# Layer 3's last output projection in row form, a two-descriptor store, and identity matmuls ahead of the last V quarter

## The chip, the cores and the metric

One core of one Trainium2 chip runs the whole program. The metric is the device time of one execution in microseconds. The span that a profile gives runs from the first to the last instruction and is 1.7 to 2.2 us shorter than that time. In the lines of a profile, PE is the matrix engine (PEld its loads of the stationary operand), DVE the vector engine, ACT the scalar engine, SPq the sync engine's DMA queue; L637 is a line of the kernel, x16 a count, and square brackets hold how long the engine idled before and what ended it. PSUM is the memory that the matmuls of this kernel write to. The granted clock is the share of its full clock that PE was given; here it is 1.00 or 0.50 at any moment.

## The reference

Four attention layers (weights and caches A, B, A, B), for one token:

```python
x = x + attention_A(layernorm(x)); x = x + attention_B(layernorm(x))     # twice
# attention: q = (x @ wq) as 32 heads of 192; scores over 8192 cached keys; softmax;
#            o = p @ v; return o.reshape(1, 1, 32 * 192) @ wo             # wo: 6144 x 640
```

All inputs are bf16; x has 640 elements. K and V of one layer are 201 MB, so the program is a stream of loads with work beside it.

## The kernel before

The heads go in 16 pairs. The output projection of a layer goes in three blocks of wo, each for five pairs; the third is split in layers 1 and 3 into a first part ("wo", 10 of 15 slices) and "wob" (5 slices), and the last pair has its own slices, "wol" (3). The sum of all of them stays in PSUM as a column block: element 5p + c of the row of 640 sits in partition p, column c. Cut to what the change touches:

```python
def busy(n):                                     # n identity matmuls, 128x128 by 128x512, result unused
    PE.wait(ev_const, last["S"][0])
    for i in range(n):
        PE.op(... matmul(SP_[0][:, :], lhsT=ident[:], rhs=ident broadcast to 512) ..., signal=False, bank=Su[0])

def project(n, w, o, ev_o):
    t3 = w.rearrange("p (i n) -> p i n", n=D)
    PE.wait(ev_o, need(n), last["YB"])
    for i in range(k):
        for c in range(DC):                      # DC = 5: one moving column each
            e = PE.op(... matmul(YB[:, c:c + 1], lhsT=t3[:, i, c:D:DC], rhs=o[:, i:i + 1], ...), bank=YBu)
# values(): in the last pair of layers 1 and 3 the second half of V comes as two quarters
            if p == NPAIR - 1 and i == rounds // 4 and quarters(("v", nl, np_, u)):
                PE.wait(need(("vq", l)))         # the last quarter of V
# end of layer 3
            return None, DV.op(lambda v: v.tensor_tensor(x_bf[:], x_true[:], YB[:, 0:DC], ALU.add), ev_y, ev_true, bank=YBu)
e = SP.op(lambda s: s.dma_start(out[0, 0].rearrange("(p c) -> p c", c=DC), x_bf[:]), ev_true, sem=semOUT, inc=16)
```

`op(..., bank=...)` makes an engine wait for the last work of every other engine on that bank. After the last V quarter these things follow, one upon another: sixteen V matmuls, two vector operations that pick the heads apart, twelve fp32 matmuls that turn the result, wob and wol, the sum with x, the store.

Of the kernel before, what the change touches and what calls it, by code (L numbers as in the profile page):

```python
# [4 lines left out]
ACT = mybir.ActivationFunctionType  # L5
ALU = mybir.AluOpType
AX = mybir.AxisListType
BF16 = mybir.dt.bfloat16
# [60 lines left out]
def build(nc, A_x, A_k, A_v, A_wq, A_wo, B_x, B_k, B_v, B_wq, B_wo, out):  # L69
    _, H, SK, DH = A_k.shape  # L70
    D = A_x.shape[-1]
    P = 128
# [25 lines left out]
    with ExitStack() as ctx:  # L98
        def sb(name, shape, dt):
            return ctx.enter_context(nc.sbuf_tensor(name, shape, dt))  # L100

        def ps(name, n=1):
            return ctx.enter_context(nc.psum_tensor(name, [P, 512 * n], F32))
# [40 lines left out]
        vs = col(1)  # L144
        rs = col(1)
        xb = sb("xb", [P, DC], BF16)

        QM = ps("QM")
        SP_ = [ps("S0"), ps("S1")]
        OY = ps("OY", 4)  # L150
        O = OY[:, 0:VK * DH]
        YB = OY[:, VK * DH:]
        TB = ps("TB")
        use = {b: {} for b in ("QM", "S0", "S1", "O", "TB", "YB")}
        QMu, Ou, TBu, YBu = [(use[b],) for b in ("QM", "O", "TB", "YB")]
# [17 lines left out]
                                        base=0, pattern=[[-1, P]], channel_multiplier=1), e)  # L173
        PO.op(lambda g: g.memset(ones[:], 1.0))
        PO.op(lambda g: g.memset(one_b[:], 1.0))
        mask = acc[:, 0:2 * VK].rearrange("p (h i) -> p h i", h=2)
        e = PO.op(lambda g: g.memset(mask, 0.0))
        for t in range(G):
# [156 lines left out]
        def quarters(n):  # L335
            return n[0] == "v" and n[2:] == (NPAIR - 1, 1) and NB[n[1]] > 0
# [51 lines left out]
        def need(n):  # L388

            while n not in landed:  # L390
                m = plan[issued[0]]
                issued[0] += 1
                landed[m] = transfer(m)
            return landed[n]
# [45 lines left out]
        def layer(l, ev_z, ev_true):  # L440
# [82 lines left out]
            def project(n, w, o, ev_o):  # L523

                t3 = w.rearrange("p (i n) -> p i n", n=D)
                k = t3.shape[1]
                PE.wait(ev_o, need(n), last["YB"])
                for i in range(k):
                    for c in range(DC):
                        e = PE.op(lambda t, i=i, c=c, f=y_first[0], fin=n[0] == "wol" and i == k - 1: t.matmul(  # L530
                            YB[:, c:c + 1], lhsT=t3[:, i, c:D:DC], rhs=o[:, i:i + 1], start=f, stop=fin,
                            skip_group_check=True), signal=(i == k - 1 and c == DC - 1), bank=YBu)
                        y_first[0] = False
                if n[0] == "wo" and (n[2] < 2 or NB[l] == 0):
                    freed[n] = e
                return e

            def columns(k):

                PE.wait(last["row_written"], last["TT"], ev_const)  # L540
                for i in range(k):
                    e = PE.op(lambda t, i=i: t.matmul(TB[:, i:i + 1], lhsT=orow[:, i:k * P:k], rhs=one_b[96:97, :],
                                                      start=True, stop=True), signal=(i == k - 1), bank=TBu)
                last["orow"] = freed[n] = e
                last["TT"] = AC.op(lambda a: a.activation(oT[:, 0:k], TB[:, 0:k], ACT.Copy),  # L545
                                   e, last["oT"], bank=TBu)
# [55 lines left out]
            def values(p, us=(0, 1)):  # L602

                par = (l * NPAIR + p) % 2
                nl, np_ = first_load("v", l, p)
                k = 2 if p == NPAIR - 1 else VK
                N = min(512, k * DH)
                PE.wait(ev_p[p])
                if 0 in us:
                    PE.wait(last["rl"])  # L610
                    if p < NPAIR - 1:
                        e = PE.op(lambda t: t.matmul(TB[96:97, C_L:C_L + 2], lhsT=ones[:, 0:1], rhs=l_col[par][:],  # L612
                                                     start=True, stop=True), bank=TBu)
                    else:
                        for h in range(2):
                            e = PE.op(lambda t, h=h: t.matmul(TB[64 * h:64 * h + 64, C_L:C_L + 1], lhsT=ones[:, 0:1].broadcast_to([P, 64]),
                                                              rhs=l_col[par][:, h:h + 1], start=True, stop=True),
                                      signal=h == 1, bank=TBu)
                    last["lc"][par] = ev_l[p] = e
                PE.wait(last["O"])  # L620
                rounds = J // k // G
                for r in range(us[0] * rounds // 2, (us[-1] + 1) * rounds // 2):
                    u, i = divmod(r, rounds // 2)
                    u = turn[nl, np_][u]
                    PE.wait(need(("v", nl, np_, u)))
                    t = slot[place[("v", nl, np_, u)]]
                    if p == NPAIR - 1 and i == rounds // 4 and quarters(("v", nl, np_, u)):
                        PE.wait(need(("vq", l)))
                    for c in range(k * DH // N):
                        for g in range(G):  # L630
                            j = (i * G + g) * k
                            o, x, y = (O[32 * g:32 * g + 2 * k, c * N:(c + 1) * N],
                                       p_sb[par][:, u * JU + j:u * JU + j + k, :].rearrange("p j h -> p (j h)"),
                                       t[:, j * DH + c * N:j * DH + (c + 1) * N])
                            f, fin = r == 0, r == rounds - 1
                            e = PE.op(lambda t, c=c, g=g, o=o, x=x, y=y, f=f, fin=fin: (
                                t.matmul(o, lhsT=x, rhs=y, start=f, stop=fin) if c == 0 else  # L637
                                matmul_held(t, o, x, y, f, fin, 32, 32 * g)),
                                signal=(fin and c == k * DH // N - 1 and g == G - 1), bank=Ou)
                if 1 not in us:  # L640
                    return
                ev_O[p] = last["p"][par] = e
                if not stays("v", l, p):
                    for u in range(2):
                        freed[("v", nl, np_, u)] = e
# [37 lines left out]
            for n in [n for n in steps if n[1] == l]:  # L683
                if n[0] == "m":
                    products(*n[2:])
                elif n[0] == "s":
                    softmax(n[2])
                elif n[0] == "v":
                    values(n[2], n[3:] or (0, 1))
                elif n[0] == "e":  # L690
                    gather(n[2])
                elif n[0] == "busy":
                    busy(n[2])
                elif n[0] == "wqr":
                    q_rows(n[2], 1)
                elif n[0] == "wq":
                    q_rows(n[2], 0, 1 if l == 2 and n[2] == 0 else None)
                    q_ready = n[2] == 2 or q_ready
                elif n[0] == "wc":
                    columns(NW)  # L700
                    last["oTw"] = last["TT"]
                elif n[0] == "wo":
                    k = NW - NB[l] if n[2] == 2 else NW
                    last["oT"] = project(n, slot[place[n]][:, 0:k * D], oT[:, 0:k], last["oTw"])
                elif n[0] == "wob":
                    last["oT"] = freed[("wo", l, 2)] = project(
                        n, slot[place[("wo", l, 2)]][:, (NW - NB[l]) * D:NW * D], oT[:, NW - NB[l]:NW], last["oTw"])
                else:
                    last["TT"] = last["TTn"]
                    last["oTl"] = ev_y = project(n, rows[:], oTl, last["TTn"])  # L710
                    if l == 1:
                        busy(2)
                if q_ready and (n[0] == "wq" and l >= 2 or n[0] == "m" and n[3] == 1):
                    following = n[2] + 1 if n[0] == "m" else 1
                    if following < NPAIR and following not in ev_q:
                        q_spread(following)
                ahead()
            if l + 1 == NL:
                return None, DV.op(lambda v: v.tensor_tensor(x_bf[:], x_true[:], YB[:, 0:DC], ALU.add), ev_y, ev_true, bank=YBu)
            ev_z = DV.op(lambda v: v.tensor_tensor(z[:], xc[:], YB[:, 0:DC], ALU.add), ev_y, ev_xc, bank=YBu)  # L720
            e = DV.op(lambda v: v.tensor_tensor(x_true[:], x_true[:], YB[:, 0:DC], ALU.add), ev_y, ev_true, bank=YBu)
            last["YB"] = e
# [1 line left out]

        for l in range(NL):
            ev_z, ev_true = layer(l, ev_z, ev_true)
        e = SP.op(lambda s: s.dma_start(out[0, 0].rearrange("(p c) -> p c", c=DC), x_bf[:]), ev_true, sem=semOUT, inc=16)
        SP.wait(e)
        assert issued[0] == len(plan)

# [51 lines left out]
```

## Time and profile before

| | before |
|---|---|
| time, median of 3 runs at first (of 6 with the later ones) | 1984.8 us (1984.76) |
| DMA engines, queue 1's share of the span | 99.5% |
| last V quarter lands | 1975.10 us |
| from there to the issue of the store | 5.43 us |
| from the issue of the store to the end of the span | 3.07 us |

The number that matters is not in any share of busy time: it is the **tail**, the 8.5 us between the landing of the last V quarter and the end of the span. All before that is set by transfers.

### The profile page before, as it was taken

How to read it: one execution, taken by the hardware profiler on the slowest of the kernel's cores; microseconds unless marked ns; L12 is line 12 of the kernel's file. 1: busy time of each engine (PE TensorE's matmuls, PEld its weight loads, DVE VectorE, ACT ScalarE, POOL GpSimd, SP SyncE). 2: the span in 40 equal slices, each digit the busy share in tenths (PEclk: the TensorE clock that was granted, in tenths of full speed). 3: DMA queues.
4: the chain of work that ended last, by engine and by line, in shares of the span. 5: the costliest groups of instructions: out<-in, count | busy, mean ns of one | idle time of the engine just before them, and what ended most of it. 6: DMA issues, size and time to landing. Idle time of an engine off the chain costs nothing.

```text
span 1983.6 us, 13955 instructions
## 1 busy us (share of the span) xinstructions
PE 1276.7 (64%) x8352; PEld 149.3 (8%) x3271; DVE 1200.5 (61%) x1371; ACT 139.5 (7%) x461; POOL 4.4 (0%) x22
## 2 busy tenths in 40 slices
PE   3567477666466665666785675665676765665657
PEld 0001001000100100100020010010002001001001
DVE  3566467467166656656745565665664774665665
ACT  0000000000000000000010000000000000000000
POOL 0000000000000000000000000000000000000000
PEclk9787777778687777787887777878886887778779
DMA  9999999999999999999999999999999999999998
GB/s 412 440 430 430 430 438 430 429 433 430 432 434 435 429 429 435 431 432 430 429 408 434 425 428 435 428 430 429 431 431 428 435 427 436 430 434 433 431 430 345
DMA packets 26926, 849.25 MB, mean 428 GB/s; under 512 B 3184, under 2 KB 3184, under 8 KB 3952
## 3 DMA queue, kind: packets, MB, share of 16 engines
q1 hardware_dynamic: 26720, 848.38, 99.5%
q8 instruction: 45, 0.74, 0.2%
q14 instruction: 17, 0.14, 0.0%
q10 hardware_dynamic: 144, 0.00, 0.0%
HBM read 848.36 MB, written 0.00 MB: 428 GB/s over the span
## 4 chain that ended last, share of the span: by engine, by line
DMA 67%; DVE 16%; PE 16%; ACT 1%; issue 0%; SPq 0%
DMA pool<-in_B_k_cache_dram 27%; DMA pool<-in_A_v_cache_dram 20%; DMA pool<-in_A_k_cache_dram 14%; DVE pool L560 14%; PE S L58 7%; DMA pool<-in_B_v_cache_dram 6%; PE OY L58 5%; PE OY L637 3%; DVE acc L656 1%; ACT p_sb L597 1%; DVE s_sb L582 1%; PE S L573 0%; PE OY L530 0%; DVE m_bf L584 0%; PE QM L587 0%
## 5 line engine op out<-in xcount | busy, mean ns | idle before, releaser
L560 DVE TENSOR_TENSOR pool<-pool,q_sb 128x3072 bf16<-128x3072 bf16 x512 | 861.1, 1754 | 241.0 <-DMA pool<-in_B_k_cache_dram 142.8
L58 PE MATMUL S<-pool,ident 128*128 128x512 bf16 x2944 | 784.6, 422 | 23.1 <-DVE pool L560 22.1
L667 PE MATMUL TB<-acc,small 128*1 128x192 f32 x240 | 80.6, 485 | 212.0 <-DVE acc L656 212.0
L573 PE MATMUL S<-pool,ident 128*128 128x512 bf16 x128 | 62.2, 486 | 213.9 <-DVE pool L560 213.9
L58 PE MATMUL OY<-pool,p_sb 128*16 128x512 bf16 x1920 | 199.7, 491 | 0.0
L655 DVE TENSOR_SCALAR acc<-OY,small 128x192 f32<-128x192 f32 x64 | 26.8, 418 | 278.0 <-PE OY L58 247.8
L637 PE MATMUL OY<-pool,p_sb 128*16 128x512 bf16 (+1 forms) x1216 | 147.0, 492 | 64.2 <-DMA pool<-in_A_v_cache_dram 57.8
L656 DVE SCALAR_TENSOR_TENSOR acc<-OY,small,acc 128x192 f32<-128x192 f32 x424 | 177.1, 418 | 14.9
L582 DVE TENSOR_REDUCE s_sb<-S 128x64 f32<-128x512 f32 x128 | 88.3, 690 | 68.6 <-PE S L58 68.6
L519 ACT ACTIVATE q_sb<-QM 128x192 bf16<-128x192 f32 x60 | 19.9, 331 | 954.7 <-PE QM L513 954.7
L678 ACT ACTIVATE rows<-TB,small 1x192 bf16<-1x192 f32 x120 | 43.2, 405 | 585.8 <-PE TB L667 585.8
L651 DVE RECIPROCAL small<-TB 1x2 f32<-1x2 f32 x64 | 11.2, 175 | 94.3 <-PE TB L612 75.3
L597 ACT ACTIVATE p_sb<-s_sb,small 64x128 bf16<-64x128 f32 x128 | 55.7, 435 | 162.2 <-DVE small L591 161.4
L573 PEld LDWEIGHTS S<-pool,ident 128*128 128x128 bf16 x128 | 12.9, 101 | 684.7 <-DVE pool L560 659.9
L612 PE MATMUL TB<-small,ones 128*1 128x2 f32 x120 | 11.4, 165 | 74.0 <-ACT p_sb L597 74.0
L637 PEld LDWEIGHTS OY<-pool,p_sb 128*16 128x16 bf16 (+1 forms) x1216 | 39.1, 106 | 206.2 <-issue 133.7
L587 PE MATMUL QM<-ident,m_bf 128*64 128x64 bf16 x128 | 14.0, 216 | 54.4 <-DVE m_bf L584 53.9
L667 PEld LDWEIGHTS TB<-acc,small 128*1 128x1 f32 x240 | 19.6, 100 | 311.0 <-DVE acc L656 284.7
L530 PE MATMUL OY<-oT,pool 128*128 128x1 bf16 x900 | 38.2, 178 | 2.8 <-ACT oT L545 2.8
L530 PEld LDWEIGHTS OY<-oT,pool 128*128 128x128 bf16 x900 | 37.1, 131 | 4.9 <-ACT oT L545 3.6
L591 DVE TENSOR_REDUCE small<-QM 128x1 f32<-128x64 f32 x64 | 14.4, 224 | 35.4 <-PE QM L587 35.4
L513 PEld LDWEIGHTS QM<-rows,one_b 1*64 1x64 bf16 x120 | 6.2, 100 | 349.4 <-issue 343.5
(62 smaller groups left out, 195.3 us busy)
## 6 DMA issues: line engine op xcount, KB each, us to landing
pool<-in_B_k_cache_dram SPq DMA_DIRECT2D x28, 6144.0 KB, 38.2
pool<-in_B_v_cache_dram SPq DMA_DIRECT2D x28, 6144.0 KB, 33.3
pool<-in_A_v_cache_dram SPq DMA_DIRECT2D x27, 6144.0 KB, 27.6
pool<-in_A_k_cache_dram SPq DMA_DIRECT2D x34, 3072.0 KB, 20.2
pool<-in_A_k_cache_dram SPq DMA_DIRECT2D x14, 6144.0 KB, 36.2
pool<-in_A_v_cache_dram SPq DMA_DIRECT2D x10, 3072.0 KB, 14.7
pool<-in_B_k_cache_dram SPq DMA_DIRECT2D x8, 3072.0 KB, 23.0
pool<-in_A_wo_dram SPq DMA_DIRECT2D x6, 2400.0 KB, 22.0
```

The lines of the kernel that those rows point to most:

```text
L58: return t.add_instruction(mybir.InstMatmult(name=t.bass.get_next_instruction_name(), engine=mybir.EngineType.PE, ins=[t.lower_ap(rhs), t. ...
L519: lambda a: a.activation(q_sb[i][:], QM[:, 0:DH], ACT.Copy), e, last["q"][i], bank=QMu)
L530: e = PE.op(lambda t, i=i, c=c, f=y_first[0], fin=n[0] == "wol" and i == k - 1: t.matmul(YB[:, c:c + 1], lhsT=t3[:, i, c:D:DC], rhs=o[:, i ...
L560: e = DV.op(lambda v, d0=d0: v.tensor_tensor(k3[:, :, d0:d0 + QD], kin[:, :, d0:d0 + QD], q_sb[qi][:, d0:d0 + QD].unsqueeze(1).broadcast_t ...
L573: t.matmul(S[:, :], lhsT=ident[:], rhs=k3[:, :, d0:d0 + R], start=True, stop=fin) if d0 == 0 else
L582: lambda v, u=u: v.tensor_reduce(s[:, u * JU:(u + 1) * JU], SP_[u][:].rearrange("p (j r) -> p j r", r=R), AX.X, ALU.add), ev_S[p, u], last ...
L597: ev_p[p] = AC.op(lambda a, h=h, r=r: a.activation(p_sb[par][r, :, h], s[r, :], ACT.Exp, bias=negm[par][r, 0:1], accum_out=l_col[par][r, h ...
L637: t.matmul(o, lhsT=x, rhs=y, start=f, stop=fin) if c == 0 else
L655: v.tensor_scalar(acc[:], O[:, 0:DH], pick[:, 0:1], None, ALU.mult) if i == 0 else
L656: v.scalar_tensor_tensor(out=acc[:], in0=O[:, i * DH:(i + 1) * DH], scalar=pick[:, i:i + 1], in1=acc[:], op0=ALU.mult, op1=ALU.add)), e if ...
L667: e = PE.op(lambda t, h=h: t.matmul(TB[96:97, C_O + h * DH:C_O + (h + 1) * DH], lhsT=half[:, h:h + 1], rhs=acc[:], start=True, stop=True), ...
L678: last["TO"] = last["row_written"] = AC.op(lambda a, h=h: a.activation(orow[:, o0 + h * DH:o0 + (h + 1) * DH], TB[96:97, C_O + h * DH:C_O ...
```

## The change

Three things, all meant for the tail: the last parts of the projection go into one row of two halves of 320 columns (partitions 0 and 32 of one bank) with o as the stationary operand, so that fewer and wider matmuls do them and the store goes out as 2 rows of 640 B instead of 128 of 10 B; the sum so far is brought from the column form into the row by three bf16 parts and identity columns; and six identity matmuls stand between the two parts of the last V half. Cut to its core:

```diff
+            def to_row(ev):                          # after the second wo block of layer 3
+                e = DV.op(... tensor_tensor(z[:], x_true[:], YB[:, 0:DC], ALU.add) ...)
+                for i in range(3):                   # three bf16 parts of z
+                    e = DV.op(... tensor_copy(part[i][:], z[:]) ...)
+                    if i < 2:
+                        e = DV.op(... tensor_tensor(z[:], z[:], part[i][:], ALU.subtract) ...)
+                PE.op(... matmul(YR, lhsT=zero[:], rhs=ident[:, 0:1] broadcast, start=True, stop=False) ...)
+                # 3 parts x 5 columns x 2 halves: matmul(YR[32*h, c:HD:DC], lhsT=part[i][:, c:c+1], rhs=ident[:, 64*h:64*h+64])
+            def project_row(n, w, o, ev_o):
+                for i in range(k):
+                    for h in range(2):
+                        e = PE.op(... matmul(YR[32 * h:32 * h + 1, :], lhsT=o[:, i:i + 1], rhs=t3[:, i, h * HD:(h + 1) * HD], ...))
 ...
+                        if l == 3:
+                            busy(6)
                         PE.wait(need(("vq", l)))
 ...   # wo part 2, wob and wol of layer 3 use project_row; to_row after wo block 1
-                return None, DV.op(lambda v: v.tensor_tensor(x_bf[:], x_true[:], YB[:, 0:DC], ALU.add), ev_y, ev_true, bank=YBu)
+                a, m = slot[place[("wo", 3, 2)]][0:33, 0:HD], 192
+                return a, (DV.op(lambda v: v.tensor_copy(a[:, 0:m], YR[:, 0:m]), ev_y, last["oT"], bank=YBu),
+                           AC.op(lambda c: c.activation(a[:, m:], YR[:, m:], ACT.Copy), ev_y, last["oT"], bank=YBu))
-        e = SP.op(lambda s: s.dma_start(out[0, 0].rearrange("(p c) -> p c", c=DC), x_bf[:]), ev_true, sem=semOUT, inc=16)
+        e = SP.op(lambda s: s.dma_start(out[0, 0].rearrange("(h n) -> h n", h=2), ev_z[0:33:32, :]), *ev_true, sem=semOUT, inc=16)
```

More of the change, by code (lines that the diff above doesn't have):

```diff
@@ L146, in build @@
         xb = sb("xb", [P, DC], BF16)
+        zero = sb("zero", [P, 33], BF16)
+        part = [sb(f"part{i}", [P, DC], BF16) for i in range(3)]
         QM = ps("QM")
@@ L152, in build @@
         YB = OY[:, VK * DH:]
+        HD = D // 2
+        YR = YB[0:33, 64:64 + HD]
         TB = ps("TB")
@@ L175, in build @@
         PO.op(lambda g: g.memset(one_b[:], 1.0))
+        PO.op(lambda g: g.memset(zero[:], 0.0))
         mask = acc[:, 0:2 * VK].rearrange("p (h i) -> p h i", h=2)
@@ L536, in project @@
                 return e
+            def to_row(ev):
+                src = z
+                e = DV.op(lambda v: v.tensor_tensor(z[:], x_true[:], YB[:, 0:DC], ALU.add), ev, ev_true, bank=YBu)
+                for i in range(3):
+                    e = DV.op(lambda v, i=i: v.tensor_copy(part[i][:], z[:]), e)
+                    if i < 2:
+                        e = DV.op(lambda v, i=i: v.tensor_tensor(z[:], z[:], part[i][:], ALU.subtract), e)
+                PE.wait(e, ev_const)
+                PE.op(lambda t: t.matmul(YR, lhsT=zero[:], rhs=ident[:, 0:1].broadcast_to([P, HD]), start=True, stop=False,
+                                         skip_group_check=True), signal=False, bank=YBu)
+                for i in range(3):
+                    for c in range(DC):
+                        for h in range(2):
+                            e = PE.op(lambda t, i=i, c=c, h=h: t.matmul(
+                                YR[32 * h:32 * h + 1, c:HD:DC], lhsT=part[i][:, c:c + 1], rhs=ident[:, 64 * h:64 * h + 64],
+                                start=False, stop=False, skip_group_check=True), signal=(i == 2 and c == DC - 1 and h == 1), bank=YBu)
+            def project_row(n, w, o, ev_o):
+                t3 = w.rearrange("p (i n) -> p i n", n=D)
+                k = t3.shape[1]
+                PE.wait(ev_o, need(n))
+                for i in range(k):
+                    for h in range(2):
+                        e = PE.op(lambda t, i=i, h=h, fin=n[0] == "wol" and i == k - 1: t.matmul(
+                            YR[32 * h:32 * h + 1, :], lhsT=o[:, i:i + 1], rhs=t3[:, i, h * HD:(h + 1) * HD], start=False, stop=fin,
+                            skip_group_check=True), signal=(i == k - 1 and h == 1), bank=YBu)
+                return e
             def columns(k):
@@ L703, in layer @@
                     k = NW - NB[l] if n[2] == 2 else NW
-                    last["oT"] = project(n, slot[place[n]][:, 0:k * D], oT[:, 0:k], last["oTw"])
+                    last["oT"] = (project_row if l == 3 and n[2] == 2 else project)(n, slot[place[n]][:, 0:k * D], oT[:, 0:k], last["oTw"])
+                    if l == 3 and n[2] == 1:
+                        to_row(last["oT"])
                 elif n[0] == "wob":
-                    last["oT"] = freed[("wo", l, 2)] = project(
+                    last["oT"] = freed[("wo", l, 2)] = (project_row if l == 3 else project)(
                         n, slot[place[("wo", l, 2)]][:, (NW - NB[l]) * D:NW * D], oT[:, NW - NB[l]:NW], last["oTw"])
@@ L709, in layer @@
                     last["TT"] = last["TTn"]
-                    last["oTl"] = ev_y = project(n, rows[:], oTl, last["TTn"])
+                    last["oTl"] = ev_y = (project_row if l == 3 else project)(n, rows[:], oTl, last["TTn"])
                     if l == 1:
```

## The prediction

> **What bounds the kernel now.** I read the page's second part first, then the chain of waits near its end, then the timeline of PE there, then the granted clock by stretch. The page says that transfers are the bound:
>
> ```profile
> PEclk9787777778687777787887777878886887778779
> DMA  9999999999999999999999999999999999999998
> ...
> q1 hardware_dynamic: 26720, 848.38, 99.5%
> ```
>
> All forty slices but the last have the DMA engines at 90% or more, and queue 1 alone took 99.5% of what 16 engines have. The change removes no byte of the 848 MB. So it can move the time only where transfers are over, in the tail, or if it starves the queue earlier. The end of the chain (start us, us, what):
>
> ```profile
> 1937.24 37.86 DMA pool<-in_B_v_cache_dram
> 1975.10 0.04 issue
> 1975.14 1.48 PE OY L637 x15
> 1976.62 0.03 issue
> 1976.64 0.43 DVE acc L655
> ...
> 1977.10 0.43 DVE acc L656
> ...
> 1977.57 1.04 PE TB L663 x12
> 1978.61 1.71 PE OY L530 x40
> ...
> 1980.34 0.16 DVE x_bf L719
> ```
>
> The last quarter of V lands at 1975.10; after it come 5.40 us of matmuls and small vector work up to 1980.50, and the output transfer closes the span at 1983.6, 3.1 us later. These 8.5 us, 0.43% of the time, are all that the change can shorten. PE around the landing, and the clock there (columns of the second: stretch, its length, busy time and count of PE, PEld, DVE, ACT, POOL, then granted clock, DMA share, GB/s):
>
> ```profile
> 1970.61 2.16 PE L530 MATMUL OY<-oT,pool 128*128 128x1 bf16 x50 [0.28 <-ACT oT L545]
> 1972.70 0.82 PE L637 MATMUL OY<-pool,p_sb 128*4 128x384 bf16 x16
> 1975.14 1.45 PE L637 MATMUL OY<-pool,p_sb 128*4 128x384 bf16 x16 [1.62 <-DMA pool<-in_B_v_cache_dram]
> ```
>
> ```profile
> 1971.30:1974.70 3.40, 2.22 (x53) 1.67 (x51) 0.00 (x0) 0.00 (x0) 0.00 (x0) 1.00 0.81 318
> 1974.70:1978.10 3.40, 1.98 (x24) 0.91 (x26) 0.84 (x2) 0.00 (x0) 0.00 (x0) 0.50 0.17 67
> 1978.10:1981.50 3.40, 2.20 (x48) 2.10 (x46) 0.16 (x1) 0.27 (x1) 0.00 (x0) 0.50 0.02 0
> ```
>
> The same sixteen V matmuls take 0.82 us before the landing and 1.45 after it: the clock fell from 1.00 to 0.50 at about 1974.7, during 1.62 us of waiting for V, and stayed at half to the end. So the whole tail runs cold.
>
> [...] In layer 1 the 3.41 us before the fall had PE "busy" for 3.13 us, but most of that was matmuls of one moving column[...]. [...] Here twelve 512-column matmuls on four column tiles take 0.645 us at clock 1.00, thus 0.215 us for each set of four[...]. [...] The trace shows 144 packets for the old one; for the new it must be seen.
>
> **The change, part by part.**
>
> *The transition (hidden).* After the second wo block of layer 3, six short vector operations split x plus the sum so far into three bf16 parts, one matmul zeroes the row and 30 matmuls of 64 columns put the parts into it. The comparable vector rows are 0.15 to 0.23 us, so about 1.3 us, and 31 matmuls at some 50 ns are 1.6: 2.9 us as an estimate. In the timeline PE ends that block at 1805.0; DVE then idles until K lands at 1809.57 and PE until 1811.4. The next transfer is issued at 1805.03, freed by the block itself and not by the new work. Cost on the path: 0.
>
> *Last wo block, first part (hidden).* 50 matmuls of one column (2.1 us, 42 ns each) become 20 of 320 columns in two column tiles: ten pairs of 320/512 x 215 = 134 ns, 1.34 us. PE gains 0.76 us ahead of a wait for V: nothing directly.
>
> *Six identity matmuls.* 6 x 0.215 = 1.29 us at full clock. PE comes to them at about 1972.7 and is free at 1974.0, before the landing at 1975.1. With the wide row matmuls, the window up to 1974.7 then holds some 2.8 us of work of many columns. I expect full clock at 1975.1. The V matmuls fall from 1.48 to 0.85 us: **-0.63**. The twelve of L663 took 0.89 us at the end of layer 0 with the clock back and 1.04 here: **-0.15**.
>
> *wob and wol.* Before, 40 matmuls of 43 ns: 1.71 us. In row form they are 5 + 3 = 8 pairs: 8 x 134 = 1.07 us plus 0.15 of drain at full clock, 1.22, that is **-0.5**; at half clock 8 x 267 + 0.15 = 2.3 us, **+0.6**. [...] about a third of the pairs warm and the rest cold, an estimate of 1.95 us, **+0.2**.
>
> *The last copy.* Before, one vector operation on 5 columns, 0.16 us. Now 192 columns on DVE and 128 on ACT. A 64-column reduction from PSUM took 0.224 us; with one element per 1.04 ns, 192 columns come to about 0.36. ACT copies 192 columns in 0.331 and 15 in 0.187, so 128 in 0.28. Both name the same bank, and the helper makes the second engine wait for the first: they run **one after the other**, 0.36 + 0.04 + 0.28 = 0.68 us, **+0.52**.
>
> *The output transfer.* 2 descriptors of 640 B for 128 of 10 B. Issue to landing was 2.7 us. The packets themselves were seen only from 1981.3 to 1981.6; 1.6 us of the rest is waiting after them. I choose **-0.3** (0 to -0.6).
>
> Sum with the clock falling at 1978.1: -0.63 - 0.15 + 0.2 + 0.52 - 0.3 = -0.4. With full clock to the end: -0.63 - 0.15 - 0.5 + 0.52 - 0.3 = -1.1. I lean a little to the second, because [...]the median is over several executions; and the issue order leaves wol's landing near 1978.2, just early enough for either. I choose **-0.9 us**: 1984.8 - 0.9 = 1983.9.
>
> **Rivals.**
> 1. *The clock falls anyway.* Six identity matmuls may not suffice, as the 1008.9 fall shows for narrow ones. Then V gains nothing, the row matmuls run at half clock: +0.6 + 0.52 - 0.3 = +0.8 us, 1985.6. Against it: in 1967.9 to 1971.3, where 32 V matmuls (1.47 us) were the only wide work, the clock stayed at 1.00.
> 2. *wol becomes the bound.* It is issued at 1970.36 and lands 7.8 us later, near 1978.2. Before, it was used at 1979.56, so 1.4 us to spare; after, about 0.2. If it comes 0.3 us later, the gain shrinks by so much. Its issue follows work that the change leaves alone.
> 3. *The identity matmuls delay V.* At half clock they take 2.6 us and end after the landing, at 1975.3 or so. Against it: the clock is 1.00 through 1974.7.
> 4. *The transfer is the gain.* If small descriptors hold back the receipt, up to 1 us more could go: 1983.0. The trace does not show what the 1.6 us after the packets is.
> 5. *The transition starves the queue.* Against it: 4.5 us of idle DVE and 6.4 of PE cover it.
>
> **Range and chances.** Three runs of before spread over 1.2 us, as much as the effect; the two clock cases and the transfer give -1.7 to +0.8. So 1982.8 to 1985.1 should hold it 8 times in 10. Two per cent is 39.7 us, five times the whole tail: faster 0.01, same 0.98, slower 0.01.
>
> **What would show it.** V's last sixteen matmuls at 0.8 us with clock 1.00 from 1975 on show the identity matmuls right; 1.45 shows them wrong. The row pairs at 134 or 267 ns tell which clock wob and wol met. The ACT copy starting only when the DVE copy ends shows the serial copies; issue to landing under 2.7 us shows the descriptor step. PE idle before wol, released by its transfer, shows rival 2. A new wait of the queue near 1805 us would show rival 5. The prediction is wrong if the clock falls before V lands, or if the landing of V itself moves by more than 1 us, which none of this explains.

The sum: it came to -0.4 us with a fall at 1978.1 and -1.1 with full clock, and -0.9 was chosen. The +0.2 is my estimate for such a fall (a third of the eight pairs at 134 ns, the rest at 267, and 0.15). That many-column work keeps the clock up was my assumption too. "The old one" with its 144 packets is the old store. What the figures can be checked with, in the trace of before unless another is named:

- The fall in layer 1 and the stretch of 3.41 us with 3.13 us of PE work belong together: granted clock 1.00 until 1008.7, then 0.50.
- 215 ns: fifteen 512-column identity matmuls took 3.40 us at clock 1.00, six 1.45, so 0.16 over 6 x 0.215, near the 0.15 of drain. The groups of twelve start 0.65 us apart (1959.50, 1960.15, 1960.80).
- 267 ns and the 2.6 us of six identity matmuls are estimates by doubling. The 16 V matmuls took 0.82 us at clock 1.00 and 1.45 at 0.50, thus 0.66 and 1.29 without that 0.16.
- 1.04 ns per column on DVE: reductions of 64 and 512 columns took 0.224 and 0.692 us.
- 50 ns for a 64-column matmul is an estimate near the 42 to 43 ns of one column; in the changed kernel 30 of them took 1.76 us at clock 0.50, 59 ns each.

## More of the kernel before

The store itself, from the sync queue's timeline (start us, us, what) and from its waits (us in total, times, longest):

```profile
1980.53 0.35 SPq L727 DMA_DIRECT2D out_dram<-x_bf  x1
SPq L98 <- DMA out_dram<-x_bf: 2.4, 1, 2.4
```

0.35 us go into the issue, then the queue waits 2.4 us for 1280 bytes to be reported written.

## The result, and the profile after

The changed kernel took **1983.58 us**, median of 6 runs (1982.41 to 1985.27), against 1984.76 us for the kernel before (6 runs, 1984.23 to 1985.38). The ratio is 0.9994 with a 95% interval of 0.9981 to 1.0007: the same by the two per cent rule, and by time alone not told apart from no change. A ratio here is the mean time of one kernel's runs over that of the other's of the same rounds, so it is not quite the ratio of the medians.

The page of the changed kernel, in the rows that the prediction showed of before:

```profile
PEclk9787777778687777777887777877886877777778
DMA  9999999999999999999999999999999999999998
...
q1 hardware_dynamic: 26580, 848.38, 99.6%
```

The bytes and the bound are the same. Its span is 1980.6 us, 3.0 less than in the profile before, but that is not the gain: here the last V quarter landed 1.2 us earlier by the luck of the stream (below). What the change can touch is the end of the chain (start us, us, what):

```profile
1936.56 37.33 DMA pool<-in_B_v_cache_dram
...
1973.92 0.85 PE OY L674 x16
...
1974.80 0.43 DVE acc L692
...
1975.25 0.43 DVE acc L693
...
1975.73 0.89 PE TB L700 x12
1976.62 1.20 PE OY L568 x16
...
1977.84 0.36 DVE pool L759
...
1978.22 0.27 ACT pool L760
```

V 1.48 to 0.85, the fp32 matmuls 1.04 to 0.89, the projection 1.71 to 1.20; then two copies, 0.65 from the first's start to the second's end, where one sum of 0.16 stood. The ACT copy starts 0.02 us after the DVE copy ends: they run one after the other. PE ahead of and at the landing, then the clock in two stretches that lie to the landing as the first two before do (columns as there):

```profile
1971.91 0.39 PE L427 MATMUL S<-ident 128*128 128x512 bf16 x1
1972.14 1.24 PE L58 MATMUL S<-ident 128*128 128x512 bf16 x5
1973.92 0.82 PE L674 MATMUL OY<-pool,p_sb 128*4 128x384 bf16 x16 [0.54 <-DMA pool<-in_B_v_cache_dram]
```

```profile
1970.10:1973.50 3.40, 3.28 (x42) 1.04 (x31) 0.00 (x0) 0.00 (x0) 0.00 (x0) 1.00 0.84 327
1973.50:1976.90 3.40, 2.00 (x34) 1.35 (x36) 0.83 (x2) 0.24 (x1) 0.00 (x0) 1.00 0.31 125
```

The identity matmuls end 0.5 us before V lands, so they delay nothing, and the second stretch is at clock 1.00 where it was 0.50. And the store:

```profile
1978.57 0.63 SPq L768 DMA_DIRECT2D out_dram<-pool  x1
SPq L98 <- DMA out_dram<-pool: 1.0, 1, 1.0
```

Its issue is longer (0.63 for 0.35), the wait after it shorter (1.0 for 2.4). From issue to end of span: 1980.6 - 1978.57 = 2.03 us, where it was 1983.6 - 1980.53 = 3.07. The packet records of the two traces show where that went. The old store ended its 144 packets (128 of 10 B, 16 of 4 B) 2.07 us before the end of the span, the new one its 4 (two of 640 B, two of 4 B) 0.72 us before; its first packet came 0.39 us later, counted from the start of the issue. So what shrank is the wait after the last packet. These 4 packets are what the prediction left to be seen. The tail is 1980.6 - 1973.88 = **6.72 us** for 8.50: -0.63 for V, -0.15 fp32, -0.51 projection, +0.49 copies, -1.04 for the store, +0.05 for the step from copy to issue, together -1.79.

The transition into the row is hidden, as PE and DVE of the changed kernel show at that place:

```profile
1806.43 0.10 PEld L552 LDWEIGHTS OY<-ident,zero 128*33 128x33 bf16 x1 [1.35 <-DVE part L548]
...
1806.82 1.76 PE L557 MATMUL OY<-ident,part 128*1 128x64 bf16 x30
1809.15 3.43 DVE L595 TENSOR_TENSOR pool<-pool,q_sb 128x3072 bf16<-128x3072 bf16 x2 [2.77 <-DMA pool<-in_B_k_cache_dram]
```

PE is done with it at 1808.6; DVE starts the next pair at 1809.15, still released by the transfer of K after 2.77 us of idling.

### The profile page after: what moved, and what is told of

Same layout as the page of the kernel before. It is cut to its first block, busy times and chain, and to the rows that moved or that the text cites. A ratio compares the mean times of both kernels' runs of the same rounds, so it can differ in the third digit from the quotient of the medians.

```text
span 1980.6 us, 13926 instructions
## 1 busy us (share of the span) xinstructions
PE 1282.8 (65%) x8335; PEld 148.6 (8%) x3249; DVE 1201.2 (61%) x1377; ACT 139.6 (7%) x462; POOL 4.5 (0%) x23
## 3 DMA queue, kind: packets, MB, share of 16 engines
q1 hardware_dynamic: 26580, 848.38, 99.6%
## 4 chain that ended last, share of the span: by engine, by line
DMA 67%; PE 17%; DVE 15%; ACT 1%; issue 0%; SPq 0%
DMA pool<-in_B_k_cache_dram 27%; DMA pool<-in_A_v_cache_dram 22%; DMA pool<-in_A_k_cache_dram 13%; DVE pool L595 13%; PE S L58 7%; DMA pool<-in_B_v_cache_dram 6%; PE OY L58 5%; PE OY L674 3%; DVE acc L693 1%; ACT p_sb L632 1%; DVE s_sb L617 1%; PE OY L535 1%; PE S L608 0%; DVE m_bf L619 0%; PE QM L622 0%
```

## The experiments

A difference of 1 us in 1984 drowns in the stream: in the fourteen profiles the last V quarter landed anywhere from 1973.69 to 1977.38 us, in kernels that issue the same loads. So the verdicts rest on the durations within the tail, which repeat to a few hundredths, and the times only check them. The table has one line for each profile. "Fall" is when the clock drops to 0.50, counted from the landing, read from granted clocks of 0.2 us slices. The parts are V matmuls, fp32 matmuls, projection, copies (or sum), and issue of the store to end of span; all in us. Spans are printed to 0.1 us, so the last two columns are good to 0.05: from the traces unrounded, the nine stores of two rows all took 2.00 to 2.01 us, the two of one row 1.54, that of 16 rows 1.74, those of 128 rows 3.05 and 3.11. The 0.82 under V in the last two lines is cut where identity matmuls follow.

Within each trace, all changes of the clock lie a whole number of steps of 3.413 us apart, to 0.01 us; in the profile of before the last four are at 1920.07, 1923.48, 1933.72 and 1974.68, thus 1, 3 and 12 steps. So the steps at which the clock did not fall can be counted back from one at which it did. Where they lie to the landing, the **phase**, differs from profile to profile.

| profile | landing | fall | V | fp32 | proj. | copy | store | tail |
|---|---|---|---|---|---|---|---|---|
| before | 1975.10 | -0.4 | 1.48 | 1.04 | 1.71 | 0.16 | 3.07 | 8.50 |
| changed kernel | 1973.88 | +4.1 | 0.85 | 0.89 | 1.20 | 0.65 | 2.03 | 6.72 |
| after_again | 1975.18 | +4.1 | 0.85 | 0.89 | 1.20 | 0.65 | 2.04 | 6.72 |
| after_c | 1974.26 | +2.4 | 0.85 | 0.94 | 2.25 | 0.65 | 1.96 | 7.74 |
| no_identity | 1976.34 | +1.2 | 0.85 | 1.04 | 2.25 | 0.65 | 1.98 | 7.86 |
| no_identity_b | 1974.17 | -0.1 | 1.48 | 1.04 | 2.25 | 0.65 | 2.02 | 8.53 |
| no_identity_c | 1974.41 | +2.0 | 0.85 | 1.01 | 2.25 | 0.65 | 2.04 | 7.89 |
| before_identity | 1973.89 | +3.1 | 0.85 | 0.89 | 1.70 | 0.16 | 3.05 | 7.71 |
| before_2x640 | 1973.89 | -0.9 | 1.48 | 1.04 | 1.71 | 0.16 | 1.98 | 7.41 |
| before_16x80 | 1977.38 | -0.7 | 1.48 | 1.04 | 1.71 | 0.16 | 1.78 | 7.22 |
| before_1x1280 | 1973.69 | -2.6 | 1.48 | 1.04 | 1.71 | 0.16 | 1.58 | 7.01 |
| parallel_copy | 1974.10 | +1.9 | 0.85 | 1.02 | 2.25 | 0.48 | 1.97 | 7.60 |
| more_identity | 1975.12 | +5.5 | 0.82 | 0.89 | 1.20 | 0.48 | 2.02 | 6.48 |
| one_row | 1974.74 | +6.6 | 0.82 | 0.89 | 1.20 | 0.48 | 1.50 | 5.96 |

### after_again and after_c: the changed kernel, twice more

No edit. My theory was that the tail is shorter by what the first profile showed; the rival, that its shorter span was luck of the stream.

> The changed kernel once more, timed closely. Theory: the tail after the last V quarter lands is 1.8 us shorter than before (6.7 against 8.5 us in the two profiles: V matmuls -0.6, fp32 transposition -0.15, row matmuls -0.5, copies +0.5, output transfer -1.05), so the median should be 1.2 to 2.0 us under the kernel before. Rival: the shorter span of the one profile was a luckier stream of loads (the last V quarter landed 1.2 us earlier there, which the change cannot cause); then the medians differ by well under 1 us and the tail in this profile is again 6.7 us.

Measured: 1983.34 us, median of 5 (1982.67 to 1983.89), against 1984.41 (9 runs); ratio 0.9994, interval 0.9981 to 1.0007. The means of the same rounds are 1983.28 and 1984.51, 1.23 us apart, as in the first set (1983.60 and 1984.72, 1.13 apart). The tail was again 6.72 us, with the landing 1.3 us later than in the first profile. So the rival is right about the span (1.2 of its 3.0 us were the stream) and wrong about the tail. The median gain, 1.07, is below the 1.2 that I expected at least.

> A third look at the changed kernel. Both looks so far had the clock at 1.00 through the row matmuls and a tail of 6.72 us. Theory: that is chance to a part, since the same identity matmuls did not prevent the fall at landing + 2.0 in the parallel-copy version; the tail is 6.72 us when a step lies within about 1.5 us after the landing and up to 7.9 us otherwise. Rival: it is always 6.72.

Measured: tail 7.74 us. The clock fell 2.4 us after the landing, in the middle of the fp32 matmuls. The chain of that run:

```profile
1974.31 0.85 PE OY L674 x16
...
1976.11 0.94 PE TB L700 x12
1977.04 2.25 PE OY L568 x15
```

The projection takes 2.25 us for 1.20, more than the 1.71 of the old column form. So the theory holds: 6.72 is the lucky case, and the three looks average 7.06, which is 1.44 less than before, whose matmul parts came out alike in all four profiles that have them (1.48, 1.04, 1.71 in the table). That is near the 1.1 to 1.2 that the times show.

### no_identity: the changed kernel without its identity matmuls

```diff
-                        if l == 3:
-                            busy(6)
                         PE.wait(need(("vq", l)))
```

> The changed kernel without the six identity matmuls. Theory: the granted clock falls to 0.5 before the last V quarter lands or close to it; the sixteen V matmuls then take 1.45 us instead of 0.82, the twelve fp32 ones 1.04 instead of 0.89, and the sixteen row matmuls 8 x 0.267 + 0.15 = 2.3 us instead of 1.2: the tail 1.9 us longer, 8.6 us, no better than before. Rival: the wide row matmuls of the last wo block alone keep the clock up; then the tail stays at 6.7 us and the identity matmuls do nothing.

Measured: 1984.79 us, median of 5 (1983.02 to 1986.01), against 1984.41 before in the same rounds, and 1.23 us more in the mean than after_again (1984.50 against 1983.28); its five runs span 3.0 us, so that difference is not clear of noise. Tail 7.86. But not as either side had it: V ran at full clock (0.85), and only what follows ran at half.

> A second look at the changed kernel without identity matmuls. In the first look the V matmuls ran at full clock (0.85 us) and the fp32 and row matmuls at half (1.04 and 2.25). Theory: the wide row matmuls of the first wo part hold the clock over the landing, and it falls after it, at a moment set by the 3.4 us steps; V 0.85 us again, rows at half clock wholly or in part. Rival: that look was lucky, and V takes 1.48 us here.

> A third look at the same kernel, for the same question: V matmuls 0.85 us by the theory, 1.48 by the rival; the tail 6.7 to 7.9 us depending on where the step lies.

Measured: V took 1.48 us in the second and 0.85 in the third; tails 8.53 and 7.89. The chain of the second:

```profile
1974.22 1.48 PE OY L672 x15
...
1976.65 1.04 PE TB L698 x12
1977.69 2.25 PE OY L568 x9
```

Both of my theories fall in part. The wide matmuls of the first wo part do not hold the clock over the landing in every run (they did in two of three), and the identity matmuls are not needed for V in every run. What is common to all three looks is that the **projection** ran at half clock, 2.25 us. In the changed kernel it ran at full clock in two looks of three (two of four with parallel_copy below, whose PE work is the same).

The average tails, 8.09 against 7.06 with three looks each, are 1.0 us apart, but the looks differ in phase too, so this is not yet the worth of the identity matmuls. Looks of like phase say more. With a step just before the landing, the clock fell without them (no_identity_b, -0.11) and held with them (one_row below, -0.20, with the same PE work up to there). With a step 2 us after the landing it fell without them (no_identity_c, +2.0) and with them (parallel_copy, +1.9), and V, fp32 matmuls and projection took the same to 0.01 us. So they pay where a step comes shortly before the landing and bring nothing where it comes 2 us after; what they are worth on the average is not shown.

### before_identity: the identity matmuls alone

```diff
+                        if l == 3:
+                            busy(6)
                         PE.wait(need(("vq", l)))
```

> The kernel before with only the six identity matmuls added between the two parts of the last V. Theory: the V matmuls after the landing take 0.85 us in place of 1.48, unless a step of the clock lies just between; the 40 one-column matmuls stay at 1.71 us whatever the clock (they took 43 ns each at clock 1.00 and 0.50), so the tail is 8.5 - 0.63 - 0.15 = 7.7 us, or 7.9 if the clock falls before the fp32 ones. Rival: [...]the clock is already down when the identity matmuls start, and they then take 2.6 us and delay V: tail 8.6 us or more.

Measured: tail 7.71 us, as the theory had it; V 0.85, fp32 0.89:

```profile
1973.94 0.85 PE OY L639 x16
...
1975.74 0.89 PE TB L665 x12
1976.63 1.70 PE OY L530 x40
```

A step lay at -0.35, and the clock held; in before it fell at a step at -0.42. So this pair differs by the identity matmuls and hardly in phase. The clock fell early in the 40 one-column matmuls, and they took 1.70 us, as before. That the old column form does not care about the clock is seen within before: 50 of these matmuls took 2.16 us at clock 1.00 and 40 took 1.71 at 0.50, 43 ns each. This small edit gives 0.79 of the tail by itself, at that phase. The row form is a bet: 0.51 us better at full clock, 0.54 worse at half.

### before_2x640, before_16x80, before_1x1280: the store alone

The kernel before, with its output taken from an unrelated buffer (wrong), after the same wait:

```diff
-  out[0, 0].rearrange("(p c) -> p c", c=DC), x_bf[:]
+  out[0, 0].rearrange("(h n) -> h n", h=2),  wq0[0][0:33:32, 0, 0:320]       # before_2x640
+  out[0, 0].rearrange("(p c) -> p c", c=40), wq0[0][0:16, 0, 0:40]           # before_16x80
+  out[0],                                    wq0[0][0:1, ...] as 640 columns  # before_1x1280
```

> The kernel before with only its last transfer changed: two rows of 640 B, taken from an unrelated buffer on purpose, so the result is wrong. Theory: the shape of the transfer alone is worth the 1.0 us: from issue to end of span 2.0 us instead of 3.07, of which the issue itself 0.63 instead of 0.35. Rival: the transfer was quicker in the changed kernel because it starts after a different instruction mix; then it stays near 3.0 us here.

> The kernel before with its output as 16 rows of 80 B from an unrelated buffer, wrong on purpose. Two rows of 640 B took 1.98 us from issue to end of span, 128 rows of 10 B 3.07. Theory: the number of descriptors counts, and 16 come close to two: about 2.0 us. Rival: [...] about 3.0 us.

> The kernel before with its output as one row of 1280 B from an unrelated buffer, wrong on purpose. Both theories[...] say 2.0 us or slightly less, as for two rows[...].

Measured, issue and wait of each in the order of the diff:

```profile
1979.32 0.63 SPq L727 DMA_DIRECT2D out_dram<-wq  x1
SPq L98 <- DMA out_dram<-wq: 1.0, 1, 1.0
```

```profile
1982.82 0.36 SPq L727 DMA_DIRECT2D out_dram<-wq  x1
SPq L98 <- DMA out_dram<-wq: 1.0, 1, 1.0
```

```profile
1979.12 0.32 SPq L727 DMA_DIRECT2D out_dram<-wq  x1
SPq L98 <- DMA out_dram<-wq: 0.8, 1, 0.8
```

Two rows wait 1.0 us in a kernel that is otherwise the old one: the shape of the store is worth 1.09 us of issue to end, whatever is in front of it. Sixteen rows of 80 B wait no longer than two of 640 B (1.0 us both), so rows of 80 B are not slow as such; the rival, 3.0 us because the rows are short, falls. The 16-row store has 16 packets of 4 B in its trace, as the old one has, so these are not what the old one waited for. One row took 0.4 us less than the 2.0 that both theories (the number of rows, or their size) gave. With 1, 2, 16 and 128 rows the waits are 0.8, 1.0, 1.0 and 2.4 us. From the last packet to the end of the span it is 0.73, 0.71, 0.73 and 2.07 us. Whether the 128 descriptors or their 10 B make the last step was not separated. The issue of two rows 32 partitions apart costs 0.63 us, that of 1, 16 and 128 neighbouring rows 0.32 to 0.36; why, stays open.

### parallel_copy: each engine copies one row

```diff
-  DVE: a[:, 0:192] <- YR[:, 0:192], bank=YBu     ACT: a[:, 192:] <- YR[:, 192:], bank=YBu
+  DVE: a[0:1, :]   <- YR[0:1, :]                 ACT: a[32:33, :] <- YR[32:33, :]
```

The rows lie on partitions 0 and 32. In the split by columns each engine read both of them and `bank=YBu` made the second wait for the first. Here each engine reads one row and the bank is no longer named, so neither waits for the other; that they may read at once was my assumption, for this run to test.

> The changed kernel with the last copy split by row instead of by columns: DVE copies 320 columns of partition 0, ACT 320 of partition 32, [...]so neither waits for the other. Theory: the copies take [...]0.49 us in place of 0.35 + 0.02 + 0.27 = 0.64: the tail 0.15 us shorter. Rival: the two engines hinder each other at the bank and it takes 0.64 us or more.

As an estimate: DVE copied 192 columns in 0.350 us (changed kernel), so 320 at 1.04 ns more for each take 0.48; ACT took 0.187 us for 15 columns and 0.331 for 192 (before), 0.81 ns each, so 0.44 for 320.

Measured: the result is correct, and the two start together (timeline):

```profile
1979.23 0.43 ACT L760 ACTIVATE pool<-OY 1x320 bf16<-1x320 f32 x1 [1.97 <-PE OY L568]
1979.23 0.48 DVE L759 CAST pool<-OY 1x320 bf16<-1x320 f32 x1 [3.35 <-PE OY L568]
```

0.48 us for 0.65, as expected: neither held the other up. The profile met an early fall of the clock (+1.9), so its tail is 7.60, not 6.57. The time is 1982.81 us, median of 5 (1982.39 to 1983.52), against 1984.41 before; ratio 0.9991, interval 0.9977 to 1.0005.

### more_identity: identity matmuls in the second gap too

```diff
+                    if l == 3 and n[2] == NPAIR - 1:
+                        busy(4)                          # while PE waits for the two DVE operations
                     gather(n[2])
```

on top of parallel_copy.

> The parallel-copy version with four more identity matmuls in the 0.95 us in which PE waits for DVE between the last V matmuls and the fp32 ones. In the traces so far the clock fell at landing + 4.1 us (changed kernel, twice), + 2.0 (parallel copy) and + 1.2 (no identity): the moment of the fall is set by where the 3.4 us steps of the clock lie. Theory: no step after the landing finds so little work now that the clock falls before the row matmuls end (landing + 3.9); they take 1.2 us, the fp32 ones 0.89, and the tail is 6.72 - 0.15 = 6.57 us; the median some 0.3 to 0.5 us under the parallel copy. Rival: the clock still falls at some step, the fp32 ones take 1.02 and the rows 2.25, tail 7.6 us, median unchanged.

Measured: clock 1.00 until the end of the projection and beyond. The stretch before the fall in parallel_copy, then two of more_identity (columns as before):

```profile
1972.67:1976.08 3.41, 1.50 (x21) 0.44 (x18) 0.83 (x2) 0.00 (x0) 0.00 (x0) 0.99 0.47 195
```

```profile
1973.80:1977.20 3.40, 2.48 (x27) 0.63 (x21) 0.84 (x2) 0.00 (x0) 0.00 (x0) 1.00 0.35 144
1977.20:1980.60 3.40, 1.83 (x28) 1.19 (x27) 0.48 (x1) 0.69 (x2) 0.00 (x0) 1.00 0.01 3
```

Projection 1.20, tail 6.48 us. A step lay at +2.06, where parallel_copy's clock had fallen at +1.94: at this phase the four matmuls held it. In the time it does not show: 1982.97 us, median of 5 (1982.65 to 1983.41), against 1982.81 for parallel_copy in other rounds, whose before was 0.2 us faster (medians 1984.41 and 1984.62). The expected 0.3 to 0.5 us are smaller than what five runs can tell, and one profile cannot show that no phase of the clock is left in which it falls.

### one_row: the output as one row

```diff
-  ACT: a[32:33, :] <- YR[32:33, :]     store: 2 rows, a[0:33:32, :]
+  ACT: a[0:1, 320:] <- YR[32:33, :]    store: 1 row,  a[0:1, 0:640]
```

on top of more_identity; ACT reads partition 32 and writes partition 0.

> The version with parallel copies and ten identity matmuls, in which ACT writes its half behind DVE's half in the same partition, so that the output leaves as one row of 1280 B. One row took 1.58 us from issue to end of span in the kernel before (wrong data), two rows 1.98 there. Theory: 1.58 here too, so the tail is 6.48 - 0.43 = 6.05 us and the median about 0.4 us under the two-row version. Rival: the two engines writing one SBUF partition, or ACT moving data from partition 32 to 0, costs as much; then the copies take over 0.9 us.

Measured: correct; copies 0.48 us still; the store:

```profile
1979.20 0.32 SPq L770 DMA_DIRECT2D out_dram<-pool  x1
SPq L98 <- DMA out_dram<-pool: 0.8, 1, 0.8
```

From issue to end 1.50 us, tail 5.96 us, 2.54 less than before and the shortest of all. Time 1982.65 us, median of 5 (1982.08 to 1984.77), against 1984.79 before; ratio 0.9991, interval 0.9978 to 1.0005. In medians and tail it beats before and the changed kernel; the interval still holds 1. Against the two-row version of more_identity the expected 0.4 us cannot be told by time (means 1983.12 and 1983.04, in different rounds); the 0.47 us (2.01 against 1.54) rest on the store's duration. It is the version that I would keep.

## Why the prediction was right

The time, 1983.58, lies 0.3 us from the predicted 1983.9 and within the range, in the class "same". That it is so near is in part luck: the six runs span 2.9 us, and two errors offset each other (below). By its steps:

- **The bound and where gain can come from**: right. The bytes, the 99.6% and the chain's head are unchanged; all that moved lies in the tail.
- **Transition, first wo part**: hidden, as said; the three lines at 1806 us show it.
- **Identity matmuls**: -0.63 came in all three looks (0.85 us), -0.15 in two (0.89; 0.94 in the third). The reason given, that they keep the clock at the landing, is shown for a step shortly before it (-0.35 held with them, -0.42 fell without), which is what the profile of before had. It is not general: without them V was at full clock in two of three looks. I had taken one profile's 1974.7 for a fixed moment; it is a matter of phase.
- **wob and wol**: both cases of the step came true in different executions. At full clock 1.20 us (said: 1.22), at half 2.25 (said: 2.3).
- **Copies**: serial, 0.65 for the 0.68 that was worked out.
- **The store**: here a size was off. The term said -0.3 (0 to -0.6); it measured -1.04 in the changed kernel and -1.09 alone. I had seen that the wait after the packets was the larger part (1.6 us by my reading) and yet assumed, with no run to show it, that most of it would stay. Rival 4, with up to 1 us more, came true in size; whether small descriptors were the cause was not separated.
- **The total**: the chosen -0.9, which lies between the sums of its two cases and follows from neither, came close since two things offset each other. The store gave 0.7 more than chosen, and the clock cost some of it back in part of the executions: the tail shrank by 1.78 or by 0.76, and the means of the timed runs differ by 1.1 to 1.2.

Rivals 2, 3 and 5 did not come about: no wait for wol's transfer and no delay of V by identity matmuls appears in any chain of the changed kernel. wol landed at about 1977.0 in its first profile and was used at 1977.2, so the 0.2 us to spare were right too. Rival 1 came about in part: V kept the clock in all looks, but in after_c the row matmuls met half clock. The range up to 1985.1 did not hold this rival's own 1985.6; nothing turned on that.

The last sign named for a wrong prediction, a landing moved by more than 1 us, did appear: 1975.10 to 1973.88. It was ill chosen. The same kernel landed at 1975.18 in after_again, and the fourteen profiles spread over 3.7 us. A small misreading: the fall in layer 1 is at the step at 1008.7 us, not 1008.9.

The timed intervals all contain 1, so that the changed kernel is faster at all is shown by the tail's parts and by two sets of rounds that agree, not by either interval alone.

## What to carry to other kernels

In a kernel bound by loads, read the tail from the last landing to the end and add up its parts; shares of busy time say nothing of it. A tiny store at the end cost 1.5 us more or less here by its shape alone, so bring the result into few rows while that work is hidden. The wide matmuls were cheaper than the many narrow ones only while the clock was up (1.20 and 2.25 us against 1.71): fill the gaps of PE in the tail, or keep the form that does not depend on it. And compare looks of like phase before you give a filler its worth.

## What the runs measured and leave open

- The time of this small store depended on its shape: 1280 B took 1.54 us as one row, 1.74 as 16 rows of 80 B, 2.00 as two of 640 B and 3.05 to 3.11 as 128 of 10 B, from issue to end of span. Why the issue of two rows 32 partitions apart takes 0.63 us, and that of the others 0.32 to 0.36, no run shows.
- PE's busy time in a step did not tell whether the clock fell at its end. In before, a step of 3.41 us with 1.44 us of PE work (1759.64 to 1763.05) ended in a fall, while one with 1.42 us (1793.77 to 1797.19, matmuls of 512 columns) did not; 3.14 us of mostly one-column matmuls (to 1008.70) ended in one as well. In parallel_copy 1.50 us ended in the fall at 1976.04, and in more_identity's tail the clock held after 2.48 us. What decides it was not shown. Where the steps lie differed from profile to profile, and with it the tail of one kernel: 6.72 or 7.74 us.
